# The last slot's V ahead of the second cache's output weights, which are loaded last, whole and in five pieces

## The chip, the cores and the metric

The kernel runs on one core of a Trainium2 chip. The metric is device time in microseconds for one execution of the whole program. Before the change the median of three runs is 2581.78 us (2581.55 to 2582.12).

## The reference

Two independent decode steps of multi-head attention with a cache (A and B), whose outputs are joined. Eight batch rows, one query token each, 32 heads of 128, 4096 cached positions, model width 1024, all in bf16.

```python
q = (x @ wq).reshape(B, Sq, H, Dh).transpose(0, 2, 1, 3)
scores = einsum("bhqd,bhkd->bhqk", q, k_cache) * Dh ** -0.5
p = softmax(scores, axis=-1)
o = einsum("bhqk,bhkd->bhqd", p, v_cache)
y = o.transpose(0, 2, 1, 3).reshape(B, Sq, H * Dh) @ wo
```

K and V of both caches are 1.07 GB together, each byte of which is used once.

## The kernel before, in words

The work is cut into 64 slots: 2 caches x 4 groups of 8 heads x 8 batch rows. One slot takes 8 heads of one batch row. Its K and its V are 8 MB each, [128 partitions x 64 KB]: 16 partitions for each head, 256 positions in each partition. K goes to one of two halves of `kbuf` (the slot's number modulo 2), V to the single `vbuf`.

For slot n, DVE multiplies K by the query in four chunks (`multiply`), PE adds the products up along the head dimension (`add_up`, 16 matmuls with the identity for each chunk), DVE finishes each chunk (`reduce`) and makes the softmax bias (`softmax`), and ACT takes the exponentials (`exps`, eight activations into `prob`). `pv` multiplies the probabilities by V: 64 matmuls in four strips of the array that accumulate in the bank `oacc`. ACT copies that bank (`copy_o`), PE collects the diagonal blocks (`gather`), and `heads` divides by the row sums into `ona`. The pv of slot m = n - 1 runs after the products of slot n.

The order on every engine is the order in which the Python code adds operations; waits are worked out from what each operation reads and writes. Slots 1 to 62 are a loop in the code of PE, ACT and DVE; slots 0 and 63 are written out. All loads are issued by SP, in the order in which they are added, and a wait of one holds those behind it.

The output projection of a cache needs all its heads. `turn_heads` and `spread_heads` put them with 128 rows on the partitions (`onp`: partition p holds rows 32p to 32p + 31 of the 4096), and `project` multiplies by the cache's output weights, which lie in `kbuf` half 0 in the same arrangement, 64 KB to a partition. It is 32 rows x 4 strips = 128 matmuls that accumulate in the bank `acc`.

At the end, slot 63, the order on SP is: K of slot 63 (half 1), the first cache's weights (half 0), V of slot 62 (`vbuf`), then after the first projection the second cache's weights (half 0 again, `load_wo(1)`), then V of slot 63 in four pieces (half 1, when the products of slot 63 have been added up), then in `vbuf` four pieces of the last head group's weights (`load_wo_last`). `load_wo(1)` takes only the first three head groups, whose heads are ready before the last slot is: 96 partitions. They are projected (`project(1)`, 96 rows of the array) between `copy_o` and `gather` of slot 62. The last group has 8 heads x 128 rows; `load_wo_last` puts one head's 128 rows on the partitions, two heads to a piece, and `project_last` uses `ona` directly, with no turning. The last piece of the last V goes to a bank of its own (`late`, with `pv_late` and a second `gather`). `idle` issues matmuls whose result nobody reads. Copies of the projection go to `orow` and from there in four stores to the output: for the first cache all on ACT, for the second two on SP and two on ACT.

The first projection stands on PE ahead of the last two `add_up` of slot 63.

Of the kernel before, what the change touches and what calls it, by code (L numbers as in the profile page):

```python
# [143 lines left out]
def _build(nc, caches, out):  # L144
# [23 lines left out]
    with es:  # L168
# [35 lines left out]
        olate = asb[:, 0:2 * Dh]  # L204
# [4 lines left out]
        wlast = vbuf[:, 0:HP * D].rearrange("p (h n) -> p h n", h=HP)  # L209
# [96 lines left out]
        def load_v(m):  # L306
            c, g, b = where(m)
            if m < NS - 1:
                dma("sp", vbuf[:], source(c, 2, b, g), ["v"], "v")
                vplace[m] = (vbuf[:], [("v", 0, T)])  # L310
                return
            i, at, parts = (NS - 1) % 2, 0, []
            for j, w in enumerate((T // 2, T // 4, T // 8, T // 8)):
                name = f"vpart{j}"
                dma("sp", kbuf[:, i, at * Dh:(at + w) * Dh], source(c, 2, b, g)[:, at * Dh:(at + w) * Dh],
                    [name] if j else [name, f"k{i}"], name)
                parts.append((name, at, w))
                at += w
            vplace[m] = (kbuf[:, i, :], parts)

        def load_wo(c):
            k = 128 if c < NC - 1 else 128 - 128 // NG
            dma("sp", kbuf[0:k, 0, :], caches[c][4][0:k * RW, :].rearrange("(p r) n -> p (r n)", r=RW), ["k0"], "wo")

        def load_wo_last():
            rows = caches[NC - 1][4][(NG - 1) * HP * Dh:, :]
            for k in range(NP):
                name = f"wlast{k}"
                dma("sp", wlast[:, 2 * k:2 * k + 2, :], rows[2 * k * Dh:(2 * k + 2) * Dh, :].rearrange("(h p) n -> p h n", p=Dh),
                    [name] if k else [name, "v"], name)  # L330
# [75 lines left out]
        def pv_part(m, part, to, bank, tb, begin, end):  # L406
            buf, parts = vplace[m]
            name, at, w = parts[part]
            per = w // tb

            def emit(e):
                last = None
                for j in range(per):
                    q, t = j % 4, at + j * tb
                    last = e.matmul(to[32 * q:32 * q + tb * HP, 0:tb * Dh],  # L415
                                    prob[:, t:t + tb, :].rearrange("p t h -> p (t h)"), buf[:, t * Dh:(t + tb) * Dh],
                                    start=(begin and j < 4), stop=(end and j >= per - 4), tile_position=(0, 32 * q))
                return last
            P.add("pe", emit, reads=[name] + probs, banks=[bank])

        def pv(m):
            wide = max(len(vplace[m][1]) - 1, 1)
            for k in range(wide):
                pv_part(m, k, oacc, "oacc", TB, k == 0, k == wide - 1)

        def pv_late(m):
            pv_part(m, len(vplace[m][1]) - 1, late, "late", 2, True, True)
            P.add("act", lambda e: e.activation(olate, late[:, 0:2 * Dh], ACTF.Copy), writes=["asb"], banks=["late"])
# [4 lines left out]
        def gather(m, after=False):  # L433
            o = 32 + (m % 2) * HP
            parts = len(vplace[m][1])
            tb, of = (2, olate) if after else (TB, osb)

            def emit(e):
                last = None
                for t in range(tb):  # L440
                    last = e.matmul(sps[:, o:o + HP], of[:, t * Dh:(t + 1) * Dh], sel[:, t, :], start=(t == 0 and not after),  # L441
                                    stop=(t == tb - 1 and (after or parts == 1)))
                return last
            P.add("pe", emit, reads=(["asb"] if after else scores) + ["sel"], banks=["sps"])
# [13 lines left out]
        def turn_heads(c):  # L458
            k = NG if c < NC - 1 else NG - 1
            for half, (t, bank) in enumerate(((bps, "bps"), (acc, "acc"))):  # L460
                def emit(e, half=half, t=t):
                    last = None
                    for j in range(4):
                        last = e.matmul(t[0:k * HP, j * Dh:(j + 1) * Dh],
                                        ona[:, c * NG:c * NG + k, :, 4 * half + j].rearrange("p g h -> p (g h)"), ident[:],
                                        start=True, stop=True)
                    return last
                P.add("pe", emit, reads=[f"ona{c * NG + g}" for g in range(k)] + ["ident"], banks=[bank])
                P.add("act", lambda e, half=half, t=t: e.activation(
                    turned[0:k * HP, 4 * half:4 * half + 4, :].rearrange("h b d -> h (b d)"), t[0:k * HP, :], ACTF.Copy),  # L470
                    writes=[f"turned{half}"], banks=[bank])

        def spread_heads(c):
            k = H if c < NC - 1 else H - HP

            def emit(e):
                last = None
                for q in range(QW):
                    last = e.matmul(bps[0:QW * k, 0:RW * B].rearrange("p (r b) -> p r b", b=B),
                                    pick[0:k, QW - 1 - q:QW - 1 - q + QW * k],  # L480
                                    turned[0:k, :, q * RW:(q + 1) * RW].rearrange("h b r -> h r b"),
                                    start=(q == 0), stop=(q == QW - 1))
                return last
            P.add("pe", emit, reads=["turned0", "turned1", "pick"], banks=["bps"])
            P.add("act", lambda e: e.activation(onp[0:QW * k].rearrange("p r b -> p (r b)"), bps[0:QW * k, 0:RW * B], ACTF.Copy),
                  writes=["onp"], banks=["bps"])

        def strips(e, vec, w, begin, end):
            last = None
            for q in range(4):  # L490
                last = e.matmul(acc[32 * q:32 * q + B, 0:CW], vec, w[:, q * CW:(q + 1) * CW], start=begin, stop=end,  # L491
                                tile_position=(0, 32 * q))
            return last

        def project(c):
            k = 128 if c < NC - 1 else 128 - 128 // NG

            def emit(e):
                last = None
                for r in range(RW):  # L500
                    last = strips(e, onp[0:k, r, :], wo[0:k, r, :], r == 0, r == RW - 1 and c < NC - 1)
                return last
            P.add("pe", emit, reads=["onp", "k0"], banks=["acc"])

        def projected():
            P.add("act", lambda e: e.activation(orow[0:104, :], acc[0:104, 0:CW], ACTF.Copy), writes=["orow"], banks=["acc"])

        def project_last():
            g = NC * NG - 1
            for k in range(NP):  # L510
                def emit(e, k=k):
                    strips(e, ona[:, g, 2 * k, :], wlast[:, 2 * k, :], False, False)
                    return strips(e, ona[:, g, 2 * k + 1, :], wlast[:, 2 * k + 1, :], False, k == NP - 1)
                P.add("pe", emit, reads=[f"ona{g}", f"wlast{k}"], banks=["acc"])
            P.add("dve", lambda e: e.tensor_copy(orow[0:104, :], acc[0:104, 0:CW]), writes=["orow"], banks=["acc"])
# [11 lines left out]
        def store(c):  # L527
            for q in range(4):
                dma("sp" if c == NC - 1 and q < 2 else "act", out[:, 0, c * D + q * CW:c * D + (q + 1) * CW],
                    orow[32 * q:32 * q + B, :], [f"out{c}{q}"], "out", reads=["orow"])  # L530

        NS = NC * NG * B
        vplace = {}
        load_wq(0)
# [11 lines left out]
        for n in range(NS):  # L546
# [19 lines left out]
            if n == NS - 1:  # L566
                turn_heads(0)
# [3 lines left out]
            if n == NS - 1:  # L571
                spread_heads(0)
                project(0)
                projected()
                store(0)
                load_wo(1)
# [3 lines left out]
            if n == NS - 1:  # L580
                turn_heads(1)
# [3 lines left out]
            if n == NS - 1:  # L585
                spread_heads(1)
            reduce(n, 3)
            softmax(n)
            if n == 0:
                make_q(1)  # L590
            if m >= 0:
# [3 lines left out]
            if n == NS - 1:  # L595
                load_v(n)
                load_wo_last()
            exps(n)
            if m >= 0:
                copy_o(m)  # L600
                if n == NS - 1:
                    project(1)
                    idle(8)
# [6 lines left out]
        idle(3)  # L610
        gather(NS - 1)
        pv_late(NS - 1)
        idle(1)
        gather(NS - 1, after=True)
        idle(1)
        heads(NS - 1)
        project_last()
        store(NC - 1)
# [100 lines left out]
```

## Time and profile before

| what | us |
|---|---|
| median of three runs | 2581.78 |
| the profiled execution's own time | 2582.06 |
| its span, first to last instruction | 2580.3 |
| PE busy | 1469.4 |
| DVE busy | 1359.5 |
| ACT busy | 651.1 |
| POOL busy | 291.2 |

The profile is one execution. Its span is 1.76 us shorter than the execution's own time. The kernel moves 1107.5 MB; the mean over the span is 429 GB/s. The page shows the span in 40 slices, with the busy share of each engine and of the DMA queues in tenths and the GB/s moved. The chain of waits is followed back from the last instruction: each line is a start, a length and what ran or was waited for. A line of the timeline is start, length, engine, source line, operation, tiles, count, and in brackets the idle time before it with what ended that.

### The profile page before, as it was taken

The numbers are of one execution on the slowest core, as the hardware profiler recorded it, in microseconds if no ns is written. First come the engines' busy times: TensorE is split into PE (matmuls) and PEld (weight loads), VectorE is DVE, ScalarE is ACT, GpSimd is POOL, SyncE is SP. The second block draws the span as 40 slices with busy tenths as digits, with TensorE's granted clock in tenths as the row PEclk, the third lists the DMA queues.
The fourth block names the chain that finished last, engine by engine and source line by source line (L and its number), as shares of the span: only waits on it lengthen the run. The fifth ranks groups of instructions, "written<-read, shape, count | busy, mean of one in ns | idle before, by whom it ended". The sixth has DMA issues, their size and how long they took to land.

```text
span 2580.3 us, 19022 instructions
## 1 busy us (share of the span) xinstructions
PE 1469.4 (57%) x9441; PEld 292.7 (11%) x5601; DVE 1359.5 (53%) x912; ACT 651.1 (25%) x1129; POOL 291.2 (11%) x112
## 2 busy tenths in 40 slices
PE   3565565555565555565565565565555565565564
PEld 0101101101101101101101101101101101101112
DVE  3556456456456456456456456456456456456450
ACT  0322322322322322322322322322322322322311
POOL 0101101101101101101101101101101101101100
PEclk8787787787787787787787787787787787787786
DMA  9999999999999999999999999999999999999999
GB/s 422 436 427 436 437 428 436 437 428 436 436 430 435 436 430 435 435 431 435 435 431 435 435 431 435 435 431 435 435 432 434 435 432 434 435 432 434 435 432 275
DMA packets 20668, 1107.53 MB, mean 429 GB/s; under 512 B 2304, under 2 KB 2368, under 8 KB 3408
## 3 DMA queue, kind: packets, MB, share of 16 engines
q1 hardware_dynamic: 20528, 1107.31, 99.9%
q8 instruction: 7, 0.11, 0.0%
q10 hardware_dynamic: 128, 0.06, 0.0%
q14 instruction: 5, 0.04, 0.0%
HBM read 1107.33 MB, written 0.03 MB: 429 GB/s over the span
## 4 chain that ended last, share of the span: by engine, by line
DMA 62%; PE 17%; DVE 14%; issue 5%; another core or an unknown queue 0%; SPq 0%; ACT 0%; DVEq 0%; ACTq 0%
DMA kbuf<-in_B_k_cache_dram 30%; DMA kbuf<-in_A_k_cache_dram 28%; PE red L364 12%; DVE kbuf L354 12%; PE oacc L415 4%; DMA kbuf<-in_B_v_cache_dram 2%; DVE osb L376 2%; DMA kbuf<-in_A_wo_dram 1%; SPq L225 0%; ACT prob L392 0%; PE acc L491 0%; DVE on L454 0%; DVEq L652 0%; PE sps L441 0%
## 5 line engine op out<-in xcount | busy, mean ns | idle before, releaser
L354 DVE TENSOR_TENSOR kbuf<-kbuf,qbc 128x8192 bf16<-128x8192 bf16 x256 | 1128.0, 4407 | 783.4 <-DMA kbuf<-in_B_k_cache_dram 390.2
L364 PE MATMUL red<-kbuf,ident 128*128 128x512 bf16 x4096 | 1049.0, 418 | 391.3 <-DVE kbuf L354 216.0
L392 ACT ACTIVATE prob<-osb,bias 128x256 bf16<-128x256 f32 x512 | 598.7, 1582 | 919.6 <-PE oacc L415 884.9
L456 POOL COPY ona<-on 128x8 bf16<-128x8 bf16 x64 | 278.7, 4355 | 2240.6 <-DVE on L454 2240.6
L441 PE MATMUL sps<-sel,osb 128*128 128x8 f32 x512 | 117.2, 358 | 648.4 <-ACT osb L431 648.4
L376 DVE TENSOR_REDUCE osb<-red 128x64 f32<-128x512 f32 x256 | 175.9, 687 | 313.8 <-PE red L364 313.8
L392 ACT ACTIVATION_READ_ACCUMULATOR prob<-osb,bias 128x1 f32 x512 | 253.0, 494 | 0.0
L346 ACT ACTIVATE qbc<-bps 128x256 bf16<-128x256 f32 x32 | 12.3, 384 | 895.8 <-PE bps L342 895.8
L415 PE MATMUL oacc<-vbuf,prob 128*32 128x512 bf16 x4032 | 231.1, 382 | 6.0 <-DMA vbuf<-in_B_v_cache_dram 6.0
L441 PEld LDWEIGHTS sps<-sel,osb 128*128 128x128 f32 x512 | 113.4, 325 | 667.9 <-issue 667.6
L364 PEld LDWEIGHTS red<-kbuf,ident 128*128 128x128 bf16 x256 | 25.2, 98 | 1182.6 <-issue 1169.2
L415 PEld LDWEIGHTS oacc<-vbuf,prob 128*32 128x32 bf16 x4032 | 102.2, 97 | 320.3 <-issue 218.0
L431 ACT ACTIVATE osb<-oacc 128x512 f32<-128x512 f32 x64 | 38.2, 598 | 38.3 <-PE oacc L415 31.2
L398 PE MATMUL sps<-rsum,ones 128*128 128x8 f32 x128 | 36.6, 360 | 5.5 <-ACT prob L392 5.5
L398 PEld LDWEIGHTS sps<-rsum,ones 128*128 128x128 f32 x128 | 34.7, 330 | 5.6 <-ACT prob L392 5.6
L454 DVE TENSOR_TENSOR on<-sps,rl 128x8 bf16<-128x8 f32 x64 | 10.1, 158 | 44.3 <-PE sps L398 44.3
L381 DVE TENSOR_REDUCE rmax<-osb 128x1 f32<-128x256 f32 x64 | 26.9, 420 | 7.6
L491 PE MATMUL acc<-kbuf,onp 128*8 128x256 bf16 (+1 forms) x256 | 12.7, 390 | 27.1 <-DMA kbuf<-in_B_wo_dram 23.3
L382 DVE STREAM_TRANSPOSE tmax<-rmax 128x32 f32<-128x32 f32 x64 | 13.5, 212 | 7.7
L383 DVE TENSOR_REDUCE nmax<-tmax 128x2 f32<-128x32 f32 x64 | 11.9, 186 | 7.6
L335 POOL COPY qg<-qT 128x256 bf16<-128x256 bf16 x32 | 12.6, 393 | 28.3 <-DVE qT L292 27.7
L385 DVE SCALAR_TENSOR_TENSOR bias<-nmax,neg 128x8 f32<-128x8 f32 x64 | 10.7, 167 | 7.7
(60 smaller groups left out, 99.5 us busy)
## 6 DMA issues: line engine op xcount, KB each, us to landing
kbuf<-in_B_v_cache_dram SPq DMA_DIRECT2D x1, 4096.0 KB, 46.1
kbuf<-in_B_v_cache_dram SPq DMA_DIRECT2D x1, 2048.0 KB, 50.6
kbuf<-in_B_v_cache_dram SPq DMA_DIRECT2D x2, 1024.0 KB, 53.6
vbuf<-in_B_wo_dram SPq DMA_DIRECT2D x4, 512.0 KB, 44.3
kbuf<-in_A_k_cache_dram SPq DMA_DIRECT2D x32, 49.3
vbuf<-in_A_v_cache_dram SPq DMA_DIRECT2D x32, 30.3
kbuf<-in_B_k_cache_dram SPq DMA_DIRECT2D x32, 49.0
vbuf<-in_B_v_cache_dram SPq DMA_DIRECT2D x31, 30.1
```

Of the source, the lines that this page charges most:

```text
L354: P.add("dve", lambda e: e.tensor_tensor(kv, kv, qbc[:, n % 2, :].unsqueeze(1).to_broadcast([128, CT, Dh]), ALU.mult), reads=[f"k{n % 2}", ...
L364: first = e.matmul(rv, ident[:], pj[:, :, 0, :], start=True, stop=False).ins
L376: P.add("dve", lambda e: e.tensor_reduce(score[:, ch * CT:(ch + 1) * CT], rv, AX.X, ALU.add), writes=[f"score{ch}"], banks=[f"red{i}"])
L381: P.add("dve", lambda e: e.tensor_reduce(rmax[:], score, AX.X, ALU.max), reads=scores, writes=["rmax"])
L382: P.add("dve", lambda e: e.transpose(tmax[:], rmax[:].to_broadcast([128, 32])), reads=["rmax"], writes=["tmax"])
L392: P.add("act", lambda e, h=h: e.activation(prob[:, :, h], score, ACTF.Exp, bias=bias[:, h:h + 1], scale=scale, accum_out=rsum[:, i, h:h + 1]),
L398: P.add("pe", lambda e: e.matmul(sps[:, i * HP:(i + 1) * HP], ones[:].to_broadcast([128, 128]), rsum[:, i, :], start=True, stop=True), rea ...
L415: last = e.matmul(to[32 * q:32 * q + tb * HP, 0:tb * Dh], prob[:, t:t + tb, :].rearrange("p t h -> p (t h)"), buf[:, t * Dh:(t + tb) * Dh] ...
L431: P.add("act", lambda e: e.activation(osb[:], oacc[:], ACTF.Copy), writes=scores, banks=["oacc"])
L441: last = e.matmul(sps[:, o:o + HP], of[:, t * Dh:(t + 1) * Dh], sel[:, t, :], start=(t == 0 and not after), stop=(t == tb - 1 and (after o ...
L456: P.add("pool", lambda e: e.tensor_copy(ona[:, gi, :, b], on[:, i, :]), reads=[f"on{i}"], writes=[f"ona{gi}"])
L491: last = e.matmul(acc[32 * q:32 * q + B, 0:CW], vec, w[:, q * CW:(q + 1) * CW], start=begin, stop=end, tile_position=(0, 32 * q))
```

## The change

V of slot 63 is one load into half 1 of `kbuf`, issued before the first projection is; `pv(63)` is 64 matmuls as in every other slot. The second cache's weights are loaded behind it as all 128 partitions, in five pieces by rows (16, 8, 4, 2 and 2 of a partition's 32 rows, so 4, 2, 1, 0.5 and 0.5 MB), each with a semaphore of its own. The last group's separate load, layout and projection are gone, as are `pv_late`, its copy and the second `gather`. The second cache's `turn_heads`, `spread_heads` and projection come after the last slot's heads, all of them for 32 heads, with `idle` matmuls (8, 5, 2, 1) between the pieces of the projection. The first cache's `turn_heads` and `spread_heads` move down by one `add_up` each, its projection behind the last one; its copy to `orow` goes from ACT to DVE.

```diff
         def load_v(m):
             c, g, b = where(m)
-            if m < NS - 1:
-                dma("sp", vbuf[:], source(c, 2, b, g), ["v"], "v")
-                vplace[m] = (vbuf[:], [("v", 0, T)])
-                return
-            i, at, parts = (NS - 1) % 2, 0, []
-            for j, w in enumerate((T // 2, T // 4, T // 8, T // 8)):
-                name = f"vpart{j}"
-                dma("sp", kbuf[:, i, at * Dh:(at + w) * Dh], source(c, 2, b, g)[:, at * Dh:(at + w) * Dh],
-                    [name] if j else [name, f"k{i}"], name)
...
+            buf, name = (vbuf[:], "v") if m < NS - 1 else (kbuf[:, m % 2, :], f"k{m % 2}")
+            dma("sp", buf, source(c, 2, b, g), [name], name)
+            vplace[m] = (buf, name)

         def load_wo(c):
-            k = 128 if c < NC - 1 else 128 - 128 // NG
-            dma("sp", kbuf[0:k, 0, :], caches[c][4][0:k * RW, :].rearrange("(p r) n -> p (r n)", r=RW), ["k0"], "wo")
-
-        def load_wo_last():
...
+            rows = caches[c][4].rearrange("(p r) n -> p r n", r=RW)
+            for j, (lo, hi) in enumerate(pieces[c]):
+                dma("sp", wo[:, lo:hi, :], rows[:, lo:hi, :], [f"wo{j}"] if j else ["wo0", "k0"], f"wo{j}")
...
+        def project(c, j):
+            lo, hi = pieces[c][j]
+
+            def emit(e):
+                last = None
+                for r in range(lo, hi):
+                    for q in range(4):
+                        last = e.matmul(acc[32 * q:32 * q + B, 0:CW], onp[:, r, :], wo[:, r, q * CW:(q + 1) * CW],
+                                        start=(r == 0), stop=(r == RW - 1), tile_position=(0, 32 * q))
+                return last
+            P.add("pe", emit, reads=["onp", f"wo{j}", "k0"], banks=["acc"])
+
+        def write_out(c):
             P.add("dve", lambda e: e.tensor_copy(orow[0:104, :], acc[0:104, 0:CW]), writes=["orow"], banks=["acc"])
...
+        pieces = [[(0, RW)], [(0, 16), (16, 24), (24, 28), (28, 30), (30, RW)]]
...
             add_up(n, 0)
-            if n == NS - 1:
-                turn_heads(0)
             multiply(n, 1)
             reduce(n, 0)
             add_up(n, 1)
             if n == NS - 1:
-                spread_heads(0)
-                project(0)
-                projected()
-                store(0)
-                load_wo(1)
+                turn_heads(0)
             multiply(n, 2)
             reduce(n, 1)
             add_up(n, 2)
             if n == NS - 1:
-                turn_heads(1)
+                spread_heads()
             multiply(n, 3)
             reduce(n, 2)
             add_up(n, 3)
-            if n == NS - 1:
-                spread_heads(1)
             reduce(n, 3)
             softmax(n)
             if n == 0:
                 make_q(1)
+            if n == NS - 1:
+                load_v(n)
+                project(0, 0)
+                write_out(0)
+                load_wo(1)
             if m >= 0:
                 pv(m)
...
-            if n == NS - 1:
-                load_v(n)
-                load_wo_last()
             exps(n)
             if m >= 0:
                 copy_o(m)
-                if n == NS - 1:
-                    project(1)
-                    idle(8)
                 gather(m)
             rowsum(n)
         heads(NS - 2)
         invert(NS - 1)
         pv(NS - 1)
         copy_o(NS - 1)
-        idle(3)
         gather(NS - 1)
-        pv_late(NS - 1)
-        idle(1)
-        gather(NS - 1, after=True)
-        idle(1)
         heads(NS - 1)
-        project_last()
-        store(NC - 1)
+        turn_heads(1)
+        spread_heads()
+        for j, k in enumerate((8, 5, 2, 1, 0)):
+            project(1, j)
+            if k:
+                idle(k)
+        write_out(1)
```

More of the change, by code (lines that the diff above doesn't have):

```diff
@@ L203, in _build @@
         score = osb[:, 0:T]
-        olate = asb[:, 0:2 * Dh]
         xs = prob[:].rearrange("p t h -> p (t h)").rearrange("p (c n) -> p c n", c=NC)
@@ L208, in _build @@
         qrow = [(asb[:].bitcast(BF16), "asb"), (osum[:].bitcast(BF16), "osum")]
-        wlast = vbuf[:, 0:HP * D].rearrange("p (h n) -> p h n", h=HP)
         red = [ps(f"red{i}", [128, 512]) for i in range(2)]
@@ L307, in load_v @@
             c, g, b = where(m)
-            if m < NS - 1:
-                dma("sp", vbuf[:], source(c, 2, b, g), ["v"], "v")
-                vplace[m] = (vbuf[:], [("v", 0, T)])
-                return
-            i, at, parts = (NS - 1) % 2, 0, []
-            for j, w in enumerate((T // 2, T // 4, T // 8, T // 8)):
-                name = f"vpart{j}"
-                dma("sp", kbuf[:, i, at * Dh:(at + w) * Dh], source(c, 2, b, g)[:, at * Dh:(at + w) * Dh],
-                    [name] if j else [name, f"k{i}"], name)
-                parts.append((name, at, w))
-                at += w
-            vplace[m] = (kbuf[:, i, :], parts)
-        def load_wo(c):
-            k = 128 if c < NC - 1 else 128 - 128 // NG
-            dma("sp", kbuf[0:k, 0, :], caches[c][4][0:k * RW, :].rearrange("(p r) n -> p (r n)", r=RW), ["k0"], "wo")
-        def load_wo_last():
[L326 to L330, printed above, removed]
+            buf, name = (vbuf[:], "v") if m < NS - 1 else (kbuf[:, m % 2, :], f"k{m % 2}")
+            dma("sp", buf, source(c, 2, b, g), [name], name)
+            vplace[m] = (buf, name)
+        def load_wo(c):
+            rows = caches[c][4].rearrange("(p r) n -> p r n", r=RW)
+            for j, (lo, hi) in enumerate(pieces[c]):
+                dma("sp", wo[:, lo:hi, :], rows[:, lo:hi, :], [f"wo{j}"] if j else ["wo0", "k0"], f"wo{j}")
         def pick_q(n):
@@ L404, in invert, with pv @@
             P.add("dve", lambda e: e.reciprocal(rl[:, i, :], sps[:, i * HP:(i + 1) * HP]), writes=[f"rl{i}"], banks=["sps"])
[L406 to L409, printed above, removed]
+        def pv(m):
+            buf, name = vplace[m]
             def emit(e):
                 last = None
[L413 to L417, printed above, removed]
-                return last
-            P.add("pe", emit, reads=[name] + probs, banks=[bank])
@@ L421, in pv @@
[L421 to L428, printed above, removed]
+                for j in range(CT):
+                    q, t = j % 4, j * TB
+                    last = e.matmul(oacc[32 * q:32 * q + TB * HP, 0:TB * Dh],
+                                    prob[:, t:t + TB, :].rearrange("p t h -> p (t h)"), buf[:, t * Dh:(t + TB) * Dh],
+                                    start=(j < 4), stop=(j >= CT - 4), tile_position=(0, 32 * q))
@@ L430, in copy_o, with gather @@
+                return last
+            P.add("pe", emit, reads=[name] + probs, banks=["oacc"])
         def copy_o(m):
             P.add("act", lambda e: e.activation(osb[:], oacc[:], ACTF.Copy), writes=scores, banks=["oacc"])
-        def gather(m, after=False):
+        def gather(m):
             o = 32 + (m % 2) * HP
-            parts = len(vplace[m][1])
-            tb, of = (2, olate) if after else (TB, osb)
             def emit(e):
                 last = None
-                for t in range(tb):
-                    last = e.matmul(sps[:, o:o + HP], of[:, t * Dh:(t + 1) * Dh], sel[:, t, :], start=(t == 0 and not after),
-                                    stop=(t == tb - 1 and (after or parts == 1)))
+                for t in range(TB):
+                    last = e.matmul(sps[:, o:o + HP], osb[:, t * Dh:(t + 1) * Dh], sel[:, t, :], start=(t == 0), stop=(t == TB - 1))
@@ L443, in emit @@
                 return last
-            P.add("pe", emit, reads=(["asb"] if after else scores) + ["sel"], banks=["sps"])
+            P.add("pe", emit, reads=scores + ["sel"], banks=["sps"])
         def heads(m):
@@ L458, in turn_heads @@
         def turn_heads(c):
-            k = NG if c < NC - 1 else NG - 1
             for half, (t, bank) in enumerate(((bps, "bps"), (acc, "acc"))):
@@ L463, in emit, with spread_heads @@
                     for j in range(4):
-                        last = e.matmul(t[0:k * HP, j * Dh:(j + 1) * Dh],
-                                        ona[:, c * NG:c * NG + k, :, 4 * half + j].rearrange("p g h -> p (g h)"), ident[:],
+                        last = e.matmul(t[0:H, j * Dh:(j + 1) * Dh],
+                                        ona[:, c * NG:(c + 1) * NG, :, 4 * half + j].rearrange("p g h -> p (g h)"), ident[:],
                                         start=True, stop=True)
                     return last
-                P.add("pe", emit, reads=[f"ona{c * NG + g}" for g in range(k)] + ["ident"], banks=[bank])
+                P.add("pe", emit, reads=[f"ona{c * NG + g}" for g in range(NG)] + ["ident"], banks=[bank])
                 P.add("act", lambda e, half=half, t=t: e.activation(
-                    turned[0:k * HP, 4 * half:4 * half + 4, :].rearrange("h b d -> h (b d)"), t[0:k * HP, :], ACTF.Copy),
+                    turned[:, 4 * half:4 * half + 4, :].rearrange("h b d -> h (b d)"), t[0:H, :], ACTF.Copy),
                     writes=[f"turned{half}"], banks=[bank])
-        def spread_heads(c):
-            k = H if c < NC - 1 else H - HP
+        def spread_heads():
             def emit(e):
@@ L478, in emit @@
                 for q in range(QW):
-                    last = e.matmul(bps[0:QW * k, 0:RW * B].rearrange("p (r b) -> p r b", b=B),
-                                    pick[0:k, QW - 1 - q:QW - 1 - q + QW * k],
-                                    turned[0:k, :, q * RW:(q + 1) * RW].rearrange("h b r -> h r b"),
+                    last = e.matmul(bps[:, 0:RW * B].rearrange("p (r b) -> p r b", b=B), pick[:, QW - 1 - q:QW - 1 - q + 128],
+                                    turned[:, :, q * RW:(q + 1) * RW].rearrange("h b r -> h r b"),
                                     start=(q == 0), stop=(q == QW - 1))
@@ L484, in spread_heads @@
             P.add("pe", emit, reads=["turned0", "turned1", "pick"], banks=["bps"])
-            P.add("act", lambda e: e.activation(onp[0:QW * k].rearrange("p r b -> p (r b)"), bps[0:QW * k, 0:RW * B], ACTF.Copy),
+            P.add("act", lambda e: e.activation(onp[:].rearrange("p r b -> p (r b)"), bps[:, 0:RW * B], ACTF.Copy),
                   writes=["onp"], banks=["bps"])
[L488 to L493, printed above, removed]
@@ L495, in project @@
-        def project(c):
-            k = 128 if c < NC - 1 else 128 - 128 // NG
+        def project(c, j):
+            lo, hi = pieces[c][j]
             def emit(e):
                 last = None
-                for r in range(RW):
-                    last = strips(e, onp[0:k, r, :], wo[0:k, r, :], r == 0, r == RW - 1 and c < NC - 1)
-                return last
-            P.add("pe", emit, reads=["onp", "k0"], banks=["acc"])
-        def projected():
-            P.add("act", lambda e: e.activation(orow[0:104, :], acc[0:104, 0:CW], ACTF.Copy), writes=["orow"], banks=["acc"])
@@ L508, in project_last @@
[L508 to L514, printed above, removed]
+                for r in range(lo, hi):
+                    for q in range(4):
+                        last = e.matmul(acc[32 * q:32 * q + B, 0:CW], onp[:, r, :], wo[:, r, q * CW:(q + 1) * CW],
+                                        start=(r == 0), stop=(r == RW - 1), tile_position=(0, 32 * q))
@@ L515, in project_last @@
+                return last
+            P.add("pe", emit, reads=["onp", f"wo{j}", "k0"], banks=["acc"])
+        def write_out(c):
             P.add("dve", lambda e: e.tensor_copy(orow[0:104, :], acc[0:104, 0:CW]), writes=["orow"], banks=["acc"])
+            for q in range(4):
+                dma("sp" if c == NC - 1 and q < 2 else "act", out[:, 0, c * D + q * CW:c * D + (q + 1) * CW],
+                    orow[32 * q:32 * q + B, :], [f"out{c}{q}"], "out", reads=["orow"])
         def idle(k):
@@ L525, in idle @@
             P.add("pe", emit, reads=["ident"], banks=["red0"])
[L527 to L530, printed above, removed]
         NS = NC * NG * B
         vplace = {}
+        pieces = [[(0, RW)], [(0, 16), (16, 24), (24, 28), (28, 30), (30, RW)]]
         load_wq(0)
```

## The prediction

> **What bounds the kernel now.** I read the page first, then the chain of waits from 2440 us on, then windows over its stages, then the timeline of the last 100 us.
>
> ```profile
> span 2580.3 us, 19022 instructions
> DMA  9999999999999999999999999999999999999999
> GB/s 422 436 427 436 437 428 436 437 428 436 436 430 435 436 430 435 435 431 435 435 431 435 435 431 435 435 431 435 435 432 434 435 432 434 435 432 434 435 432 275
> ```
>
> The queues look busy in every slice, and 39 slices move 422 to 437 GB/s. The last slice (64.5 us) moves only 275 while its busy digit is still 9: something there keeps the queues occupied without moving bytes. That slice is the place of the change. The chain of waits:
>
> ```profile
> 2467.36 33.85 DMA kbuf<-in_A_wo_dram
> 2501.34 6.21 PE acc L491 x99
> ...
> 2515.33 46.13 DMA kbuf<-in_B_v_cache_dram
> ...
> 2561.50 1.91 PE oacc L415 x32
> ...
> 2566.39 1.05 PE oacc L415 x16
> ...
> 2568.87 1.05 PE oacc L415 x8
> ...
> 2577.59 0.42 DVE orow L515
> ```
>
> The first cache's weights land at 2467.36 + 33.85 = 2501.21, the last V's first half only at 2515.33 + 46.13 = 2561.46; in the 60 us between them slot 62's V and the second cache's 96-partition weights land. From the timeline:
>
> ```profile
> 2481.87 4.43 DVE L354 TENSOR_TENSOR kbuf<-kbuf,qbc 128x8192 bf16<-128x8192 bf16 x1 [12.29 <-DMA kbuf<-in_B_k_cache_dram]
> 2523.13 5.56 PE L415 MATMUL oacc<-vbuf,prob 128*32 128x512 bf16 x64 [6.05 <-DMA vbuf<-in_B_v_cache_dram]
> 2551.98 6.21 PEld L491 LDWEIGHTS acc<-kbuf,onp 96*8 96x8 bf16 x128 [23.78 <-issue]
> 2515.33 1.76 SPq L225 DMA_DIRECT2D kbuf<-in_B_v_cache_dram  x4
> 2497.11 4.41 DVE L354 TENSOR_TENSOR kbuf<-kbuf,qbc 128x8192 bf16<-128x8192 bf16 x1
> 2511.62 3.63 PE L364 MATMUL red<-kbuf,ident 128*128 128x512 bf16 x16
> ```
>
> K of slot 63 has landed when its multiply starts, 2481.83 (0.04 us before it). So the first weights, 128 partitions of 64 KB (8.39 MB), took 2501.21 - 2481.83 = 19.38 us, 433 GB/s; slot 62's V landed at 2523.1, 21.9 us later, and the 96-partition weights (6.29 MB) at 2551.9, another 28.9 us: 218 GB/s. The windows say the same (columns: stretch, length, each engine's busy time and count, granted clock, DMA share, GB/s):
>
> ```profile
> 2482.00:2501.00 19.00, 12.63 (x51) 2.45 (x21) 18.21 (x8) 1.45 (x3) 4.42 (x1) 0.77 0.99 425
> 2521.00:2549.00 28.00, 5.56 (x64) 2.05 (x64) 0.00 (x0) 9.96 (x17) 0.00 (x0) 0.62 0.97 208
> 2552.00:2562.00 10.00, 9.81 (x158) 6.51 (x162) 0.28 (x2) 0.00 (x0) 0.22 (x1) 0.71 0.96 411
> 2570.00:2574.00 4.00, 4.00 (x28) 2.55 (x26) 0.00 (x0) 0.77 (x2) 0.00 (x0) 0.50 1.04 385
> ```
>
> The load into 96 partitions runs at half rate with the queues 97% occupied. That load sets the pace of the last 60 us, and no engine does: PE's weight loads stand 23.8 us before it is there.
>
> **The change part by part.**
>
> *The transfers.* The last slot's V (one issue) now stands in SP's queue ahead of the second cache's weights. It waits for the last add_up alone, which no longer stands behind the first projection (2501.34 to 2507.55). Slot 63's last product ends at 2497.11 + 4.41 = 2501.5; behind it on PE stand the rest of spread_heads (1.88 us, row below) and the last add_up (3.63), so V is issued by about 2507 instead of at 2515.33. The first projection (3.1 to 6.2 us) follows it on PE, then the five weight issues, 1.76 / 4 = 0.44 us each, by 2516. Slot 62's V occupies the queues until about 2520, so they never run dry. Write_out's copy, now on DVE, and its four issues on ACT fall near 2512, when both are idle.
>
> Slot 62's V: 2501.21 + 19.38 = 2520.59; the 2.5 us that it came later than this in before fall, as I read it, to packets of the 96-partition load that started beside its last ones, and are gone. Slot 63's V: 2539.97. For the weights in pieces, before's V is the price, cut in the same way with the same 64 KB row pitch: its second piece (2 MB) landed at 2566.35 and the third (1 MB) at 2568.83 (each 0.04 before the PE rows above), 4.89 and 2.48 us. So 4 MB is 9.7, 2 MB 4.89, 1 MB 2.48. Pieces of 0.5 MB with 4 KB runs are nowhere in the trace: below at 433 GB/s 1.21, above at the 385 of the stretch with 2 KB runs 1.36; I take 1.28. The landings: 2549.7, 2554.6, 2557.0, 2558.3, 2559.6.
>
> Before's last landing:
>
> ```profile
> L225 SPq DMA_DIRECT2D vbuf<-in_B_wo_dram x4: 368/430/10920, 2528.8 to 2541.0; - x4
> DMA to landing us min/median/max: 35.6/44.3/45.6
> ```
>
> 2541.0 + 35.6 = 2576.6. The stream is 17.0 us shorter, for the same 16.8 MB behind slot 62's V. The 10.92 us in which SP stood at one of these issues had up to 6 + 32 + 48 packets (one to a partition's run, over 16 engines) queued with it; the new order has at most 8 + 8 + 40, and were SP to stand, work would still be queued.
>
> *PE's tail.* It gets turn_heads, spread_heads and all 128 projection matmuls of the second cache behind the last V, where before only 32 matmuls stood; removed are pv_late with its copy and gather, and the 96-row work. The rows:
>
> ```profile
> 2571.10 1.72 PE L441 MATMUL sps<-sel,osb 128*128 128x8 f32 x8
> 2575.38 0.19 DVE L451 TENSOR_TENSOR ona<-sps,rl 128x8 bf16<-128x8 f32 x1 [13.74 <-PE sps L441]
> 2491.46 0.46 PE L464 MATMUL bps<-ident,ona 128*32 128x128 bf16 x4
> 2492.45 0.57 ACT L469 ACTIVATE turned<-acc 32x512 bf16<-32x512 f32 x1
> 2495.65 1.88 PE L479 MATMUL bps<-turned,pick 32*128 32x256 bf16 x4
> 2497.57 0.38 ACT L485 ACTIVATE onp<-bps 128x256 bf16<-128x256 f32 x1 [4.55 <-PE bps L479]
> 2558.41 1.90 PE L523 MATMUL red<-ident 128*128 128x512 bf16 x8
> 2569.85 1.46 PE L523 MATMUL red<-ident 128*128 128x512 bf16 x3
> 2538.20 0.60 ACT L431 ACTIVATE osb<-oacc 128x512 f32<-128x512 f32 x1
> ```
>
> pv of slot 62 at 2520.63 for 5.56, as before: 2526.2. From that end to the copy's start took 2538.20 - 2528.69 = 9.5 (the eight exponentials), then 0.60 and the gather 1.72: 2538.0, with one rowsum behind it, ahead of V at 2539.97. pv of slot 63 the same 5.56: 2545.6. Copy 0.1 + 0.60 + 0.1: 2546.4; gather: 2548.1; heads with its two hops 0.36: 2548.5; turn_heads to the end of its second copy, 2493.02 - 2491.46 = 1.56: 2550.0; spread_heads and copy, 2497.95 - 2495.65 = 2.30: 2552.3. From there 128 matmuls at 6.21 / 128 = 0.049 and 16 idle ones at 1.46 / 3 = 0.49 would be 14.0 at half clock. At full clock an idle one costs 1.90 / 8 = 0.24; with the projection halved likewise it is 6.9, ending at 2559.2, under the transfers. So at full clock the last landing decides, and the end is 2559.6 + 0.04 + 8 matmuls 0.4, + 0.05 + copy 0.42, + the stores, 2580.3 - 2578.01 = 2.29: 2562.8.
>
> That is 17.5 us off the span. The profiled execution took 2582.06, 1.76 outside its span; the median is 2581.78, 0.28 below it. So 2562.8 + 1.76 - 0.28 = 2564.3 if the transfers decide to the end.
>
> The clock can make it later. Slot 62's pv ran 3.9 us before it was granted full clock, the 96-row projection 5.8 us:
>
> ```profile
> 2523.00:2527.07 4.07, 3.94 (x40) 1.51 (x44) 0.50 0.84 177
> 2555.00:2557.80 2.80, 2.80 (x60) 1.89 (x56) 0.50 0.96 404
> 2557.80:2558.10 0.30, 0.30 (x20) 0.25 (x16) 1.00 1.52 655
> ```
>
> If gather, turn and spread (thin work; the window 2570 to 2574 stayed at 0.50 with PE busy throughout) let it fall, the last stretch costs half clock for x = 3.9 to 5.8 us and then half of what is left: x + (14.0 - x) / 2 = 9.0 to 9.9, ending at 2561.3 to 2562.2, 1.3 to 2.2 after the transfers' 2560.0. The idle matmuls count in this, since they stand in order ahead of the next piece. The trace does not settle whether it falls, so between 0 and 2.2 I take 0.9: **2565.2**.
>
> [...]
>
> **The rivals.**
> *PE ends last, at low clock.* If pv of slot 63 is wholly at half clock, 64 x 3.94 / 40 = 6.3, the start moves to 2553.0, and with x = 5.8 the stretch ends at 2562.9, 2.9 later than the transfers: 2567.2. If the full clock is never granted it ends at 2567.0: 2571.3. For it: the low clock from 2570 on. Against it: pv is dense work, and both dense stretches of the trace were granted full clock within 5.8 us.
> *The half rate belongs to the second cache's weights, not to the 96 partitions.* Then 8.39 MB at 218 GB/s take 38.5 us behind 2539.97: 2578.5 and 3.2 of tail, 2581.7 in span, 2583.2: slower than before. It turns from faster to slower at about 2577.1 for the last landing, 226 GB/s. Against it: the same tensor's last group ran at 385 GB/s into 128 partitions; for it: that was another part of the tensor, in 2 KB runs.
> *Each of the pieces pays a fixed cost.* The row with such a cost is the stores at the end, 2.29 us for 4 KB each; four more such costs are 9.2 us: 2573.5. Against it: the 0.07 us a piece of before's V, which was queued in the same way.
> *The order doesn't change what the queues do*, since V and weights sum to the same bytes: then 2581.8, as before. Against it: the stretch at 208 GB/s goes with the 96-partition load.
>
> **How the numbers follow.** Transfers decide, with PE up to 2.2 us late (2564.3 to 2566.5): 0.78. PE's low clock, 2566.5 to 2568.5: 0.10. Fixed cost a piece, 2573: 0.04. Half rate kept, 2583: 0.05. No change: 0.03. The range 2563.2 to 2568.5 takes the first two and the 0.15 us on each small piece, with 1 us below for a shorter store. A measurement of this kernel tells about 0.2%, 5 us, from no change: faster holds the first three, 0.92; same 0.06 (no change and most of the half rate); slower by more than 5 us needs a rate below 206 GB/s, 0.02.
>
> **What would show it.** The last 60 us at 400 GB/s or more and no stretch near 210; slot 62's V landing at about 2520.6 and slot 63's at 2540; wo pieces 4.9, 2.5, 1.3, 1.3 us apart; the chain's last transfer the fifth piece, with its eight matmuls right behind. It is wrong in the clock if PE has no idle time before the last pieces, in the rate or the pieces if the last weights land after 2565.

## The result, and the profile after

| | median, us | runs |
|---|---|---|
| before | 2581.76 | 6, 2581.48 to 2582.12 |
| after | 2566.78 | 6, 2565.99 to 2567.21 |

The ratio is 0.9942, 95% interval 0.9929 to 0.9955: 15.0 us faster. The forecast was 2565.2, in a range of 2563.2 to 2568.5. The profiled execution took 2566.77, its span 2565.0. The page of the profile after:

```profile
span 2565.0 us, 18933 instructions
GB/s 425 431 435 432 434 434 432 436 430 438 429 437 429 437 429 437 430 436 430 436 431 435 431 435 432 434 432 434 432 434 433 434 432 435 431 435 431 435 432 377
```

The last slice moves 377 GB/s where before it moved 275; the other 39 lie between 425 and 438 (before: 422 to 437). The windows over the end after (columns as before: stretch, length, PE, PE's weight loads, DVE, ACT and POOL busy, granted clock, DMA share, GB/s):

```profile
2521.00:2549.00 28.00, 15.45 (x153) 7.95 (x146) 0.47 (x3) 10.61 (x19) 0.22 (x1) 0.68 0.97 418
2549.00:2558.00 9.00, 7.80 (x96) 3.59 (x97) 0.00 (x0) 1.39 (x3) 0.00 (x0) 0.64 0.95 394
2558.00:2560.00 2.00, 2.00 (x41) 0.94 (x37) 0.00 (x0) 0.00 (x0) 0.00 (x0) 1.00 0.16 61
```

The same 28 us that moved 208 GB/s before move 418, at the same DMA share of 0.97: the share says how long packets were under way, not what they moved. A window counts a packet whole where it starts, so by 2558 nearly all of them have started. The chain of waits after shows what came last:

```profile
2506.26 33.62 DMA kbuf<-in_B_v_cache_dram
2539.88 0.04 issue
2539.92 6.29 PE oacc L396 x61
...
2550.06 1.90 PE bps L445 x4
2551.96 0.02 issue
2551.99 0.39 ACT onp L450
2552.38 0.04 issue
2552.42 3.40 PE acc L460 x63
2555.82 1.83 PE red L477 x8
2557.66 0.98 PE acc L460 x32
2558.63 1.19 PE red L477 x5
2559.82 0.54 PE acc L460 x16
2560.36 0.54 PE red L477 x2
2560.90 0.32 PE acc L460 x8
2561.22 0.32 PE red L477
2561.54 0.35 PE acc L460 x8
2561.89 0.03 DVEq L578
2561.92 0.04 issue
2561.97 0.43 DVE orow L466
```

Slot 63's V lands at 2539.88. From there to the end the chain has no transfer in it: PE goes from piece to idle matmuls (L477) to piece without a wait. The five weight pieces were there each time, and PE was what ended last.

### The profile page after: what moved, and what is told of

It reads as the page before. It is cut to its first block, busy times and chain, and to the rows that moved or that the text cites. A ratio compares the mean times of both kernels' runs of the same rounds, so it can differ in the third digit from the quotient of the medians.

```text
span 2565.0 us, 18933 instructions
## 1 busy us (share of the span) xinstructions
PE 1465.7 (57%) x9400; PEld 289.2 (11%) x5560; DVE 1360.2 (53%) x913; ACT 650.2 (25%) x1127; POOL 291.1 (11%) x112
## 4 chain that ended last, share of the span: by engine, by line
DMA 62%; PE 18%; DVE 13%; issue 6%; SPq 0%; another core or an unknown queue 0%; DVEq 0%; ACT 0%; ACTq 0%
DMA kbuf<-in_B_k_cache_dram 31%; DMA kbuf<-in_A_k_cache_dram 30%; PE red L347 12%; DVE kbuf L337 11%; PE oacc L396 5%; DVE osb L359 2%; DMA kbuf<-in_B_v_cache_dram 1%; SPq L223 0%; PE acc L460 0%; DVE on L423 0%; PE red L477 0%; DVEq L593 0%; PE bps L445 0%; PE oacc L275 0%
## 5 line engine op out<-in xcount | busy, mean ns | idle before, releaser
L396 PE MATMUL oacc<-vbuf,prob 128*32 128x512 bf16 x4032 | 231.2, 382 | 10.8 <-DMA vbuf<-in_B_v_cache_dram 10.8
L275 PE MATMUL oacc<-vbuf,orow 128*8 128x512 bf16 x64 | 7.2, 440 | 11.8 <-DMA vbuf<-in_A_wq_dram 11.8
```

The source lines that it names most:

```text
L396: last = e.matmul(oacc[32 * q:32 * q + TB * HP, 0:TB * Dh], prob[:, t:t + TB, :].rearrange("p t h -> p (t h)"), buf[:, t * Dh:(t + TB) * D ...
```

## The experiments

Nine kernels were run. Each time below is to be held against the kernel before (medians of 2581.9 to 2582.0 beside these runs) and the changed kernel (2566.78).

**1. The rate alone, in the order of before.**

```diff
         def load_wo(c):
-            k = 128 if c < NC - 1 else 128 - 128 // NG
+            k = 128
```

> The kernel before with one edit: the second cache's early weights are loaded into all 128 partitions (8.39 MB) though only 96 are used, everything else and the order as before. My theory (the 96-partition load runs at half rate): the load takes 19.4 us instead of 28.9, the last V part lands near 2559.5 instead of 2571.3, and with before's 9.1 us of tail the span is about 2568.6, the time about 2570.4, 11 us faster though 2.1 MB more are moved. Rival (the order was the gain): not faster, about 2586.6 for the extra 2.1 MB.

Measured: 2570.55 (4 runs, 2570.37 to 2570.65), ratio to before 0.9955 (0.9940 to 0.9971). One stage of its windows and two steps of its chain of waits:

```profile
2520.00:2540.00 20.00, 5.60 (x64) 2.12 (x64) 0.00 (x0) 9.96 (x17) 0.00 (x0) 0.67 0.98 425
```

```profile
2515.38 42.05 DMA kbuf<-in_B_v_cache_dram
2557.42 0.04 issue
2557.47 1.05 PE oacc L415 x8
```

The stretch that crawled now runs at 425 GB/s, with two megabytes more to load, and a piece of the last V that landed at 2568.83 before lands at 2557.42: 11.4 us, and the time falls by 11.5. Three quarters of the change's gain come from a load that fills all partitions, with the order left alone.

**2. The order alone.**

```diff
             if n == NS - 1:
-                load_v(n)
                 project(0, 0)
                 write_out(0)
                 load_wo(1)
+                load_v(n)
```

> The changed kernel with the last slot's V issued behind the five weight pieces instead of ahead. My theory: the stream is as long as in the changed kernel, but V lands last, near 2559.3, and the 12.5 us from V's landing to onp and the 9.5 us of projection stand behind it: span about 2584.4, time about 2586.2. Rival (only the rate of the load matters, not the order): 2566.8.

Measured: 2586.04 (10 runs, 2585.60 to 2586.62), ratio to before 1.0015 (1.0005 to 1.0024). The chain of waits of this kernel:

```profile
2512.68 47.03 DMA kbuf<-in_B_v_cache_dram
2559.71 0.04 issue
2559.76 5.45 PE oacc L396 x34
...
2570.93 0.39 ACT onp L450
2571.32 0.04 issue
2571.36 3.59 PE acc L460 x64
...
2582.15 0.42 DVE orow L466
```

The last bytes arrive about as early as in the changed kernel, but they are V's, and 22.4 us of dependent work stand behind them: 11.6 to `onp` and 10.8 of projection. With the new tail and without the new order the kernel is 4.0 us slower than before, though its loads are whole: in a kernel that has this tail, the order is worth 2586.04 - 2566.78 = 19.3 us. Part of that price is the idle matmuls between the pieces, which take 2.88 + 1.19 + 0.54 + 0.32 = 4.9 us of this chain and cost only 1.8 us in the changed kernel (run 3). Without them in either kernel the order would be worth about 16 us, an estimate from these numbers.

**3. Without the idle matmuls between the pieces.**

```diff
-        for j, k in enumerate((8, 5, 2, 1, 0)):
+        for j, k in enumerate((0, 0, 0, 0, 0)):
```

> The changed kernel without the 16 idle matmuls between the pieces of the last projection. My theory (PE ends last, since the clock fell to half and the idle matmuls stand in order): the projection follows the landings, the last matmul ends near 2560.0 instead of 2561.9, time about 2564.9. Rival (the transfers decide the end already): 2566.8. Second rival (without idle matmuls the pieces at half clock take as long): 2566 to 2567.

Measured: 2564.95 (5 runs, 2564.88 to 2565.22), ratio to before 0.9934 (0.9921 to 0.9948). Its timeline, matmuls and the copy behind them:

```profile
2552.53 4.20 PE L460 MATMUL acc<-kbuf,onp 128*8 128x256 bf16 x96 [0.47 <-ACT onp L450]
...
2557.15 0.61 PE L460 MATMUL acc<-kbuf,onp 128*8 128x256 bf16 x16 [0.42 <-DMA kbuf<-in_B_wo_dram]
...
2558.39 0.39 PE L460 MATMUL acc<-kbuf,onp 128*8 128x256 bf16 x8 [0.62 <-DMA kbuf<-in_B_wo_dram]
...
2559.61 0.39 PE L460 MATMUL acc<-kbuf,onp 128*8 128x256 bf16 x8 [0.83 <-DMA kbuf<-in_B_wo_dram]
2560.11 0.42 DVE L466 CAST orow<-acc 104x256 bf16<-104x256 f32 x1 [11.71 <-PE acc L460]
```

Now PE waits for each of the last three pieces, and the copy starts at 2560.11 instead of 2561.97. This is the fastest kernel of the study, 1.8 us under the changed one, and its runs don't overlap with that one's. The 16 idle matmuls had stood ahead of pieces that had landed.

**4. More idle matmuls, to hold the clock.** Two behind the last pv, three behind turn_heads, two behind spread_heads, where PE waits for ACT; the others as in the changed kernel. The number that `turn_heads` and `spread_heads` take is that of the idle matmuls issued at their end.

```diff
         copy_o(NS - 1)
+        idle(2)
         gather(NS - 1)
         heads(NS - 1)
-        turn_heads(1)
-        spread_heads()
+        turn_heads(1, 3)
+        spread_heads(2)
```

> The changed kernel with 7 more idle matmuls where PE waits for ACT: 2 behind the last pv, 3 behind turn_heads, 2 behind spread_heads of the second cache. My theory: the granted clock stays full to the projection, its first piece takes 1.8 us instead of 3.4, PE is ahead of the last landing: last matmul near 2560.0, time about 2564.9. Rival (the clock goes by dense work in its own windows, or the idle matmuls delay the chain): 2566.5 to 2567.5.

Measured: 2566.88 (5 runs, 2565.89 to 2567.02), no gain over the changed kernel. Its windows:

```profile
2548.00:2552.00 4.00, 3.58 (x17) 1.22 (x17) 0.19 (x1) 1.27 (x3) 0.00 (x0) 0.98 0.93 395
2552.00:2556.00 4.00, 4.00 (x68) 2.16 (x67) 0.00 (x0) 0.18 (x1) 0.00 (x0) 0.59 0.97 403
```

The first of these stretches in the changed kernel:

```profile
2548.00:2552.00 4.00, 2.88 (x13) 1.04 (x12) 0.19 (x1) 1.08 (x3) 0.00 (x0) 0.58 0.94 401
```

My expectation failed, and its rival came out. The idle matmuls did keep the clock up for longer, 0.98 where the changed kernel was granted 0.58. But it fell at the end of these 4 us, just as the projection began (0.59 over the next 4 us), though PE had been busy for 3.58 of them; the first piece took 3.23 us against 3.40. So these seven do not hold it into the projection (whether more would was not tried), and a PE that the profile shows busy was not enough to hold it, nor to raise it: in the kernel before it stayed at 0.50 from 2570 to 2574 with PE busy throughout.

**5. What a load into part of the partitions costs.** In the changed kernel the first weight piece (16 rows, 4 MB) is split by partitions; here for 96 + 32:

```diff
             for j, (lo, hi) in enumerate(pieces[c]):
+                if c == 1 and j == 0:
+                    dma("sp", wo[0:96, lo:hi, :], rows[0:96, lo:hi, :], ["wo0", "k0"], "wo0")
+                    dma("sp", wo[96:128, lo:hi, :], rows[96:128, lo:hi, :], ["wo0b"], "wo0b")
+                    continue
...
-            P.add("pe", emit, reads=["onp", f"wo{j}", "k0"], banks=["acc"])
+            P.add("pe", emit, reads=["onp", f"wo{j}", "k0"] + (["wo0b"] if c == 1 and j == 0 else []), banks=["acc"])
```

> The changed kernel with its first weight piece (4 MB, 16 rows) loaded as two transfers: partitions 0 to 95, then 96 to 127. My theory (a load into 96 partitions runs at half rate, 218 GB/s, and so does one into 32): 14.4 + 4.8 us instead of 9.7, every later landing 9.5 us later, time about 2574.3. [...] Rival (the half rate had to do with the order or with what ran beside it in the kernel before): 2566.8.

> As the run with 96 + 32 partitions, but 64 + 64. If the partitions reached set the rate, each half runs at 218 GB/s: 9.6 + 9.6 us instead of 9.7, time about 2574.4. If only a number of partitions that 128 is no multiple of is slow: 2566.8.

> As the run with 96 + 32 partitions, but 112 + 16. [...]

One run each: 2577.34 (96 + 32), 2577.60 (64 + 64), 2578.74 (112 + 16). A stretch in which the split piece loads, in that order (mostly the first of its two transfers; with 64 + 64, some of each):

```profile
2543.00:2553.00 10.00, 7.89 (x80) 3.42 (x72) 0.19 (x1) 1.66 (x3) 0.00 (x0) 0.84 1.03 208
```

```profile
2543.00:2553.00 10.00, 8.07 (x82) 4.00 (x75) 0.19 (x1) 1.66 (x3) 0.00 (x0) 0.67 1.01 211
```

```profile
2543.00:2553.00 10.00, 7.68 (x76) 3.27 (x64) 0.19 (x1) 1.83 (x4) 0.00 (x0) 0.84 1.05 247
```

The half rate comes back in a kernel that has the new order, at the same place in the stream, with the same source rows and the same queue. It goes with the split and with nothing else of the kernel before. With 96 + 32 and 64 + 64 the times came out 3.0 and 3.2 us above the expectation for half rate; the timeline of 96 + 32 shows most of the rest:

```profile
2542.07 5.29 PE L400 MATMUL oacc<-kbuf,prob 128*32 128x512 bf16 x64 [3.24 <-DMA kbuf<-in_B_v_cache_dram]
...
2562.83 3.41 PE L464 MATMUL acc<-kbuf,onp 128*8 128x256 bf16 x64 [9.75 <-DMA kbuf<-in_B_wo_dram]
```

V of slot 63, a full load ahead of the split one, landed at 2542.03 instead of 2539.88. With 64 + 64 it landed at 2542.48, with 112 + 16 at 2541.53. So the slow load cost the one before it 1.7 to 2.6 us too, as slot 62's V had lost 2.5 in the kernel before.

**6. Which partitions, or how many.** The same 64 + 64 partitions, but the middle ones first; the projection again waits for all parts.

```diff
+                if c == 1 and j == 0:
+                    for i, (a, b) in enumerate(((32, 96), (0, 32), (96, 128))):
+                        dma("sp", wo[a:b, lo:hi, :], rows[a:b, lo:hi, :], [f"wo0{i}"] if i else ["wo0", "k0"], f"wo0{i}" if i else "wo0")
+                    continue
...
-            P.add("pe", emit, reads=["onp", f"wo{j}", "k0"], banks=["acc"])
+            P.add("pe", emit, reads=["onp", f"wo{j}", "k0"] + (["wo01", "wo02"] if c == 1 and j == 0 else []), banks=["acc"])
```

> As the run with 64 + 64 partitions, but the first piece is loaded as partitions 32 to 95, then 0 to 31, then 96 to 127. If the rate goes by which partitions are reached (0 to 63 and 64 to 127 being two halves with ways of their own), the middle 64 run at the full rate, 4.9 us, the two 32s at half rate, 4.8 us each: 14.5 us instead of the 19 of 64 + 64, time about 2573. If any load into fewer than 128 partitions runs at half rate or less: as 64 + 64 or later, 2577.6 or more.

One run: 2573.63. Its windows, two single microseconds in the first transfer and one at its end, and a stretch in the next two:

```profile
2540.00:2541.00 1.00, 1.00 (x12) 0.37 (x16) 0.00 (x0) 0.00 (x0) 0.00 (x0) 0.50 1.06 459
2541.00:2542.00 1.00, 1.00 (x12) 0.33 (x8) 0.00 (x0) 0.00 (x0) 0.00 (x0) 0.50 1.00 393
2542.00:2543.00 1.00, 1.00 (x16) 0.46 (x12) 0.00 (x0) 0.00 (x0) 0.00 (x0) 0.50 2.15 393
```

```profile
2546.00:2554.00 8.00, 4.08 (x32) 1.90 (x20) 0.19 (x1) 2.04 (x4) 0.00 (x0) 0.70 1.01 211
```

Partitions 32 to 95 load at the full rate, 459 and 393 GB/s in the first two rows at shares near 1; 0 to 31 and 96 to 127 at half, 211 GB/s in the last row. In the third row packets of the next transfer already start: its share of 2.15 shows that they take longer for as many bytes. It is which partitions are reached, not that there are fewer than 128: 64 of them that lie half below 64 and half above load at the full rate here, while the lower 64 and the upper 64, each in a transfer of its own, ran at about 211 GB/s in run 5.

That the time met the expected 2573 is in part luck. From V's landing to the projection it took 17.8 us against 20.3 with 64 + 64, a gain of 2.5 us where 4.5 was expected (14.5 against 19). V itself landed 2.6 us earlier, at 2539.86, as no slow load stood right behind it.

**7. The weights in one piece**, without idle matmuls.

```diff
-        pieces = [[(0, RW)], [(0, 16), (16, 24), (24, 28), (28, 30), (30, RW)]]
+        pieces = [[(0, RW)], [(0, RW)]]
...
-        for j, k in enumerate((8, 5, 2, 1, 0)):
+        for j, k in enumerate((0,)):
```

> The changed kernel with the second cache's weights in one piece of 8 MB and no idle matmuls. My theory: the last landing stays near 2559.3, then all 128 matmuls stand behind it, at half clock since PE has been idle for 7 us: 6.4 us, time about 2570.6. [...]

Measured: 2569.80 (4 runs, 2569.40 to 2570.39), ratio to before 0.9953 (0.9937 to 0.9970). The chain of waits:

```profile
2510.35 49.05 DMA kbuf<-in_B_wo_dram
2559.40 0.14 issue
2559.54 5.58 PE acc L460 x125
2565.12 0.04 DVEq L578
```

The one piece lands at 2559.40; the last of five landed at 2559.57 in run 3 (0.04 before its matmuls). Counted from V's landing (2539.84 here, 2540.02 in run 3) that is 19.56 and 19.55 us. Four more pieces cost at most 0.2 us of transfer together, and save the 5 us in which all 128 matmuls stand behind the last byte.

## Why the prediction was right, step by step

*What bounds.* Right: the load into 96 partitions at half rate, shown by run 1 (whole, the loss is gone) and by run 5 (split, it is back). What the forecast called the rival on the other side, half rate kept by the second cache's weights, fell with the 394 GB/s of 2549 to 2558 after, in which these weights load and no V does.

*The transfers.* The landings were right to about 0.1 us. Slot 62's V landed at 2520.53 (2520.59 forecast), without the 2.5 us of before. V of slot 63 was issued at 2506.26 (about 2507 forecast) and landed at 2539.88 (2539.97). In run 3, where PE waits for them, the last three pieces landed at 2557.11, 2558.35 and 2559.57; forecast 2557.0, 2558.3, 2559.6. The 4 KB runs that the trace of before did not show were within the bounds given: 1.22 to 1.24 us for half a megabyte, 423 to 430 GB/s, near the full rate.

*The fixed cost of a piece.* In the trace of before, pieces of the last V of 2 and 1 MB landed in 4.89 and 2.48 us, which leaves 2 x 2.48 - 4.89 = 0.07 us for a piece. That held: with pieces queued behind each other, run 7 against run 3 leaves at most 0.2 us for four of them. The 2.29 us of the stores at the end, which the rival took for such a cost, did not add up here.

*PE's tail.* Right in its length, off in two terms that cancelled: pv of slot 63 took 6.25 us (5.56 forecast), mostly at half clock (granted 0.50 from 2539.9 to 2545), but in its last part the full clock was granted (1.00 from 2545.4), and the gather took 1.03 instead of 1.72 (granted 1.00 from 2547.0 to 2548.1). The projection began at 2552.42 (2552.3).

*The clock.* This is the term that was mis-sized. By the forecast's own sign it was wrong here: PE had no idle time before the last pieces, and the chain's last transfer is V, not the fifth piece. The median of 2566.78 lies just inside the band of the rival "PE ends last, at low clock" (2566.5 to 2568.5), which had a chance of 0.10, and not in the one that had 0.78. The forecast put PE's lateness between 0 and 2.2 us and took 0.9, as the trace left open whether the clock falls. It fell: the first piece ran at half clock, 3.40 us, and the copy started at 2561.97 against 2560.11 when the transfers decide (run 3), 1.86 us late, near the upper bound. That is 1.0 of the 1.3 us by which the span exceeded 2562.8 + 0.9 = 2563.7. The other 0.3 is the store: 2565.0 - 2562.40 = 2.6 us, where 2.29 was taken from before. That the upper bound held is in part luck, as two errors cancelled: the projection ran at half clock for about 3.1 us (granted 0.50 from 2550 to 2555 and 0.92 from 2555 to 2558), not for 3.9 to 5.8, but at full clock (1.00 from 2555.5 on) its matmuls did not halve. The second piece's 32 took 0.98 us, 0.031 each, where half of 0.049 was assumed. That the idle matmuls count on this path, as the forecast said, is shown by run 3; that the seven of run 4 would hold the clock is refuted by that run.

*The order.* The forecast gave it no price of its own: it made V's landing early and asked only whether PE would be hidden behind the weights. Run 2 gives the price, 19.3 us in this kernel (some 3 of them through the idle matmuls), and run 1 shows that the old order with a whole load gets 11.5 of the 15.0 us.

Two things stay open. Why 96 and 112 partitions, which reach beyond the lower 64, load at 208 to 247 GB/s rather than in the time of their fuller half (96: with 64 of them at half of 433 GB/s, 433 / 2 x 96 / 64 = 325 GB/s, an estimate) was not tried. The trace of before shows only that the slowness is not confined to the lower 64: the 64 KB packets that start from 2520.3 to 2546.2 all take 4.7 to 5.1 us, against 2.42 in a whole load (slot 63's V after). And what the clock counts is not known; a PE that the profile shows busy was not enough (0.50 from 2570 to 2574 in the kernel before).

## What to carry to other kernels

A queue can be busy and move half (208 GB/s at a DMA share of 0.97 in the kernel before): compare GB/s with the DMA share, and where they part, look at which partitions the load reaches. Leaving out the last quarter of the partitions of a large load saved a quarter of the bytes and made it take 28.9 us instead of 19.4. When a stream ends a kernel, put last in it what has the least work behind it, in pieces that shrink toward the end, and let nothing on the engine, not even matmuls meant for the clock, stand ahead of a piece that has landed (1.8 us here, run 3).

## What the runs showed of the hardware that was not expected

- A load into partitions 32 to 95 ran at the full rate (459 and 393 GB/s in two microseconds of run 6), loads into 0 to 63 and 64 to 127 at about 211 (run 5).
- A load into 96 partitions ran at 208 GB/s (run 5), no faster than one into 64 (211).
- A load at half rate delayed the full-rate load queued ahead of it, by 1.7 to 2.6 us in run 5.
- The granted clock fell at the end of 4 us in which PE was busy 3.58 (run 4; 0.98 in them, 0.59 in the next 4), with eight matmuls of 128 columns, four on 32 rows and five idle ones. In the kernel before it stayed at 0.50 from 2570 to 2574 with PE busy throughout, fp32 matmuls with 8 columns among others.
